# A fused attention and two-layer feed-forward kernel: VectorE in emission order after the attention, the second layer's block sums in the accumulators, the first layer's last products added by DMA

## The chip, the cores and the metric

One core of one Trainium2 chip. The metric is the device time of one execution in microseconds (us). The engines are TensorE (PE; its weight loads are PEld), VectorE (DVE), ScalarE (ACT), GpSimd (POOL) and SyncE (SP), which here only issues DMAs; POOL issues DMAs too, those that add to their target among them.

## The reference

```python
scores = scale * np.matmul(q, k.transpose(0, 1, 3, 2))         # 2 x 8 heads, 768 tokens, 64 wide
...                                                             # bias by distance, local and global keys kept
a = np.exp(scores - max); a = a / (a.sum(-1) + 1e-09)
x = np.matmul(a, v) -> reshaped to (1536, 512)
h = x @ w_in;  x = (h * (1 / (1 + np.exp(-h)))) @ w_out         # layer 0: 512 -> 2048 -> 512
h = x @ w_in2; out = (h * np.clip(h + 3, 0, 6) / 6) @ w_out2    # layer 1: 512 -> 2048 -> 512
```

The weights lie in memory as 64-bit floats.

## The kernel before

**Numbers.** Every matmul operand is split into a high half in a reduced 32-bit format (made by ACT) and a low half, the rest (made by DVE), and every product is three matmuls: high by high, high by low, low by high. A weight is loaded raw by SP (tile `raw`, two buffers) and *decoded* into a 32-bit float by a chain of small steps in 128x512 pieces: absolute value on ACT (L103), then on DVE clamp, shift, sign, power (L987 to L1004), scale (L129), add (L134), then the high half on ACT (L145) and the low half on DVE (L148). The load of the piece after the next is issued when a piece has been scaled.

**Stages.** The attention fills the first 130 us or so, and the first chunk of the feed-forward runs between its matmuls. Each layer is cut into 8 *chunks* of 256 hidden columns, written (layer, chunk). The 1536 tokens are three *blocks* of 512. An *H piece* (`h_piece`, 12 matmuls) gives 128 hidden rows for one block; ACT and DVE make the gated value and its halves from it (`gate_tile`: activation L529/L531, gate L536, `gh` L539, `gl` L542). A *Y piece* (`y_piece`, 6 matmuls) multiplies it by `w_out`; its results are summed over the chunks in the accumulators `acc[l, i]` (tiles `y0`, `y1`, `y2`): ACT copies a result to a staging tile `st` (three buffers, two results each), and POOL issues a DMA that adds it to `y` (L685). The last chunk of layer 0 is added by DVE instead (L695), and its sums are scaled and split into `xh` and `xl`, the input of layer 1.

**Fast chunks.** An ordinary chunk computes the H values of blocks 0 and 1 in 48 matmuls. A *fast* chunk needs 42: seven products of six matmuls (`product`, banks `psP_a`, `psP_b`, `psP_c`) of sums of weight quarters (`sums`) and sums of token blocks. The latter are made once per layer by `block_sums`: four differences of 128x1024 (L632), two on DVE (`V`) and two on POOL (`G`), and the halves T2, T3, T4 of three results, and a fourth that is written over the input of block 1. They work on whole copies of blocks 0 and 1 (`whole_blocks`, tiles `xf`), in layer 0 the sum of the two halves by two DMAs (SP, then an adding one on POOL), in layer 1 a copy of the accumulator. In a fast chunk two products are combined by DVE's addition into `u` (L595).

**Order.** The program is one list, `stream`, of H pieces, products and Y pieces, one per loop step `n`; the Y pieces of a block stand between the H pieces or products of a later one. `at(n, f)` puts an operation ahead of step n, `rests` and `late` put one behind it, `slots` holds the decode steps at fixed distances ahead of the chunk that needs the weights. PE, ACT and POOL work in just the order in which this loop emits (`manual_schedule`); DVE's and SP's orders are chosen by the library's scheduler from the dependencies. Each engine takes its instructions strictly in its order and waits at one whose inputs are not there.

```python
def fast(l, c):
    return c > (2, 0)[l]
...
for l, c, loop in ((0, 1, 5), (1, 0, 1)):
    if n == when(first_piece[l, c]) + loop:
        block_sums(l, n, when(first_piece[l, c + 2 - l]) - 7)
```

So layer 0 makes its block sums in chunk (0,1), and all chunks of layer 1 but the first are fast.

## Time and profile before

| | us |
|---|---|
| runs | 657.25, 653.9, 656.02; median 656.02 |
| the profiled execution | 653.48 |
| its span, first to last instruction | 651.7 |
| PE busy | 620.8 (95%) |
| DVE busy | 538.4 (83%) |
| ACT busy | 413.1 (63%) |
| POOL busy | 166.3 (26%) |
| mean granted clock of PE | 0.990 |

Shares of busy time are means over stages with different limits, so the views below are cut to stretches. A timeline gives start, duration, engine, line, operation, what is written and read, and in brackets the idle time of the engine before it and what ended that. Rows of one engine overlap a little at their ends: what an operation costs its engine is the distance from its start to the next one's.

### The profile page before, as it was taken

How to read it: one execution, taken by the hardware profiler on the slowest of the kernel's cores; microseconds unless marked ns; L12 is line 12 of the kernel's file. 1: busy time of each engine (PE TensorE's matmuls, PEld its weight loads, DVE VectorE, ACT ScalarE, POOL GpSimd, SP SyncE). 2: the span in 40 equal slices, each digit the busy share in tenths (PEclk: the TensorE clock that was granted, in tenths of full speed). 3: DMA queues.
4: the chain of work that ended last, by engine and by line, in shares of the span. 5: the costliest groups of instructions: out<-in, count | busy, mean ns of one | idle time of the engine just before them, and what ended most of it. 6: DMA issues, size and time to landing. Idle time of an engine off the chain costs nothing.

```text
span 651.7 us, 9793 instructions
## 1 busy us (share of the span) xinstructions
PE 620.8 (95%) x3208; PEld 500.2 (77%) x3208; DVE 538.4 (83%) x1173; ACT 413.1 (63%) x885; POOL 166.3 (26%) x229
## 2 busy tenths in 40 slices
PE   5989999999699999999999996999999999999996
PEld 3657777788588778888888884778888888888885
DVE  5899889945977888979887999989979797979553
ACT  4787778743555666666666653856757576666760
POOL 2776666662211111111111012001111211111110
PEclk9999999999899999999999997999999999999999
DMA  7555645358367668777777540235877677776544
GB/s 172 131 145 140 140 125 127 87 181 159 77 150 162 139 152 187 177 174 165 169 162 159 132 162 33 65 97 134 186 166 175 160 183 166 168 172 135 104 98 165
DMA packets 80762, 94.17 MB, mean 145 GB/s; under 512 B 55360, under 2 KB 55360, under 8 KB 80448
## 3 DMA queue, kind: packets, MB, share of 16 engines
q0 software_dynamic: 11424, 39.85, 34.0%
q1 hardware_dynamic: 69280, 53.63, 27.4%
q8 instruction: 27, 0.44, 0.3%
q14 instruction: 31, 0.25, 0.1%
HBM read 46.27 MB, written 3.15 MB: 76 GB/s over the span
## 4 chain that ended last, share of the span: by engine, by line
PE 74%; DVE 15%; DMA 6%; issue 2%; ACT 1%; SPq 1%; POOL 1%; POOLq 0%; DVEq 0%; ACTq 0%
PE psY L666 33%; PE psH L510 15%; PE psP_b L578 6%; PE psP_a L578 4%; PE psP_c L578 4%; PE psS L388 3%; PE psT L416 3%; PE psO L435 3%; PE psA L331 2%; DMA xf<-xl 2%; DMA xf<-xh 1%; DVE xl L607 1%; DVE da L999 1%; DMA raw<-in_moe_w_in_dram 1%; DVE gl L542 1%
## 5 line engine op out<-in xcount | busy, mean ns | idle before, releaser
L685 POOL DMA_DIRECT2D y<-st x72 | 61.7, 857 | 366.1 <-ACT st L682 356.3
L682 ACT COPY st<-psY 128x512 f32<-128x512 f32 x144 | 84.6, 587 | 57.3 <-PE psY L666 51.7
L510 PE MATMUL psH<-xh,wih 128*128 128x512 f32 (+1 forms) x200 | 76.8, 384 | 0.0
L510 PE MATMUL psH<-xh,wil 128*128 128x512 f32 (+1 forms) x200 | 76.2, 381 | 0.0
L510 PE MATMUL psH<-xl,wih 128*128 128x512 f32 (+1 forms) x200 | 76.2, 381 | 0.0
L666 PE MATMUL psY<-gh,woh 128*128 128x512 f32 (+1 forms) x160 | 62.1, 388 | 2.9 <-ACT gh L539 2.9
L666 PE MATMUL psY<-gl,woh 128*128 128x512 f32 (+1 forms) x160 | 61.5, 384 | 2.4 <-DVE gl L542 2.4
L539 ACT CAST gh<-g 128x512 fp32r<-128x512 f32 (+1 forms) x74 | 45.3, 612 | 25.9 <-DVE g L536 25.8
L666 PE MATMUL psY<-gh,wol 128*128 128x512 f32 (+1 forms) x160 | 61.1, 382 | 0.0
L398 ACT ACTIVATE z<-z,mn 128x256 f32<-128x256 f32 (+1 forms) x96 | 46.5, 486 | 22.0 <-DVE mn L394 17.4
L407 POOL TENSOR_SCALAR z<-z,sm 128x256 f32<-128x256 f32 (+1 forms) x96 | 48.3, 517 | 44.2 <-DVE sm L405 16.1
L666 PE MATMUL psY<-woh,gh 128*128 128x512 f32 x136 | 53.9, 396 | 5.6 <-ACT gh L539 5.5
L542 DVE TENSOR_TENSOR gl<-g,gh 128x512 fp32r<-128x512 f32 (+1 forms) x68 | 46.6, 685 | 11.1 <-ACT gh L539 10.5
L536 DVE SCALAR_TENSOR_TENSOR g<-a,psH 128x512 f32<-128x512 f32 (+1 forms) x50 | 33.1, 662 | 26.7 <-ACT a L529 17.8
L666 PE MATMUL psY<-woh,gl 128*128 128x512 f32 x136 | 53.8, 395 | 0.9 <-DVE gl L542 0.8
L666 PE MATMUL psY<-wol,gh 128*128 128x512 f32 x136 | 53.6, 394 | 0.0
L103 ACT ACTIVATE da<-raw 128x512 f32<-128x512 f32 x64 | 43.0, 671 | 5.2 <-DMA raw<-in_moe_w_in_dram 5.2
L987 DVE TENSOR_SCALAR da<-da 128x512 f32<-128x512 f32 x64 | 30.6, 479 | 18.7 <-ACT da L103 18.7
L529 ACT ACTIVATE a<-psH 128x512 f32<-128x512 f32 (+1 forms) x30 | 17.1, 570 | 44.8 <-PE psH L510 44.8
L999 DVE SCALAR_TENSOR_TENSOR da<-raw,da 128x512 int32<-128x512 int32 x64 | 44.3, 693 | 1.4 <-DVE sm L404 0.2
L510 PEld LDWEIGHTS psH<-xh,wih 128*128 128x128 f32 x200 | 37.6, 188 | 7.8 <-issue 1.0
L510 PEld LDWEIGHTS psH<-xh,wil 128*128 128x128 f32 x200 | 37.5, 188 | 6.6
(170 smaller groups left out, 1607.1 us busy)
## 6 DMA issues: line engine op xcount, KB each, us to landing
y<-st POOLq DMA_DIRECT2D x72, 512.0 KB, 5.0
raw<-in_moe_w_in_dram SPq DMA_DIRECT2D x32, 512.0 KB, 4.1
raw<-in_moe_w_out_dram SPq DMA_DIRECT2D x32, 512.0 KB, 4.7
rk<-in_k_dram SPq DMA_DIRECT2D x32, 96.0 KB, 2.6
rq<-in_q_dram SPq DMA_DIRECT2D x32, 96.0 KB, 3.1
rv<-in_v_dram SPq DMA_DIRECT2D x32, 96.0 KB, 2.7
out_dram<-y SPq DMA_DIRECT2D x12, 256.0 KB, 2.0
xf<-xh SPq DMA_DIRECT2D x2, 1024.0 KB, 6.7
```

Source lines behind the costliest of these rows:

```text
L103: nc.scalar.activation(out=t["a"], in_=raws[n][:, :, 1].bitcast(F32), func=AF.Abs)
L398: nc.scalar.activation(out=z[:, h, :w], in_=z[:, h, :w], func=AF.Exp, bias=mn[:, h:h + 1], scale=-1.0, accum_out=sm[:, h:h + 1])
L407: nc.gpsimd.tensor_scalar(out=z[:, h, :w], in0=z[:, h, :w], scalar1=sm[:, h:h + 1], scalar2=1.0, op0=ALU.mult, op1=ALU.mult)
L510: nc.tensor.matmul(ps, a[:, kt, js], x[:, kt, n0:n1], start=n == 0, stop=n == 3 * KT - 1)
L536: nc.vector.scalar_tensor_tensor(out=g, in0=t["a"], in1=ps, op1=ALU.mult, **op)
L539: nc.scalar.copy(gh[:, j, :], t["g"])
L542: (nc.vector if ready[0] else nc.gpsimd).tensor_tensor(out=gl[:, j, :], in0=t["g"], in1=gh[:, j, :].bitcast(F32), op=ALU.subtract)
L578: nc.tensor.matmul(ps, a[:, 2 * k + q, f * P:(f + 1) * P], x, start=p in (1, 5) and n == 0, stop=n == 5, skip_group_check=True)
L666: nc.tensor.matmul(ps[:, :rhs.shape[1]], lhs, rhs, start=n == 0, stop=n == 3 * FC - 1)
L682: nc.scalar.copy(st[:, m % 2, :], part)
L685: late.setdefault(now[0] + 1, []).append(lambda: nc.gpsimd.dma_start(y, st, accum_op=ALU.add))
L999: nc.vector.scalar_tensor_tensor(out=ai, in0=w1, scalar=-0x40000000, in1=ai, op0=ALU.bitwise_and, op1=ALU.bitwise_or)
```

## The change

DVE, too, works in emission order from the end of the attention on. The block sums of layer 0 are made in chunk (0,2) instead of (0,1), those of layer 1 in chunks (1,0) and (1,1), all on DVE; layer 1's are made in the old accumulators themselves, and the first sums of the new accumulators are held in the two large tiles until then and copied over by `first_sums`. So chunk (1,1) is an ordinary one. Layer 0's last products go through `st` and the adding DMA as all others do, and a pair of results is scaled and split 6 to 3 steps later. At the layer change the pieces stand in a new order.

```diff
@@ -154,7 +154,7 @@
 
     def fast(l, c):
 
-        return c > (2, 0)[l]
+        return c > (2, 1)[l]
 
     terms = {}
 
@@ -612,34 +612,38 @@
             at(n, first)
         at(n + 1, second)
 
-    def whole_blocks(l, b):
-
-        T[l, b] = late_pool.tile([P, KT, FB], F32, name=f"xf{l}{b}", tag=("ws", "g1")[b])
-        if l == 0:
-            h, o = (x.bitcast(F32)[:, :, b * FB:(b + 1) * FB] for x in (xh, xl))
-            nc.sync.dma_start(T[l, b], h)
-            nc.gpsimd.dma_start(T[l, b], o, accum_op=ALU.add)
-        else:
-            nc.sync.dma_start(T[l, b], acc[0, b])
+    def whole_block(b):
+
+        T["x", b] = late_pool.tile([P, KT, FB], F32, name=f"xf{b}", tag=("g1", "ws")[b])
+        h, o = (x.bitcast(F32)[:, :, b * FB:(b + 1) * FB] for x in (xh, xl))
+        nc.sync.dma_start(T["x", b], h)
+        nc.gpsimd.dma_start(T["x", b], o, accum_op=ALU.add)
 
     def block_sums(l, n, n1):
 
-        b0, b1 = T[l, 0], T[l, 1]
+        b0, b1 = (T["x", b] if l == 0 else acc[0, b] for b in range(2))
         b11, b12, b21, b22 = b0[:, :2, :], b1[:, :2, :], b0[:, 2:, :], b1[:, 2:, :]
         for k in (2, 3, 4):
             T[k] = [late_pool.tile([P, 2, FB], F32R, name=f"t{k}{x}{l}", tag=f"t{k}{x}") for x in "hl"]
         t1 = late_pool.tile([P, 2, FB], F32, name=f"t1f{l}", tag="u")
-        tt = lambda e, out, a, b: e.tensor_tensor(out=out, in0=a, in1=b, op=ALU.subtract)
-        V, G = nc.vector, nc.gpsimd
+        sub = lambda out, a, b: nc.vector.tensor_tensor(out=out, in0=a, in1=b, op=ALU.subtract)
         scale = (1.0, 0.5)[l]
-        at(n, lambda: tt(V, t1, b12, b11))
-        at(n + 1, lambda: tt(V, b11, b22, t1))
-        at(n + 2, lambda: tt(G, b12, b22, b12))
-        at(n + 3, lambda: tt(G, b21, b21, b11))
-        split(n + 3, *T[2], b11, scale)
-        split(n + 5, *T[3], b12, scale)
-        split(n + 7, *T[4], b21, scale)
+        at(n, lambda: sub(t1, b12, b11))
+        at(n + 2, lambda: sub(b12, b22, b12))
+        at(n + 3, lambda: sub(b11, b22, t1))
+        split(n + 4, *T[3], b12, scale)
+        split(n + 6, *T[2], b11, scale)
+        at(n + 8, lambda: sub(b21, b21, b11))
+        split(n + 9, *T[4], b21, scale)
         split(n1, *(x[:, :2, FB:2 * FB] for x in (xh, xl)), t1, scale)
+        if l:
+            at(n + 10, first_sums)
+
+    def first_sums():
+
+        for b in range(2):
+            acc[1, b] = xpool.tile([P, FB // P, DM], F32, name=f"y1_{b}", tag=f"y{b}")
+            nc.gpsimd.dma_start(acc[1, b], T["y", b])
 
     def parts(n0, n1):
 
@@ -667,6 +671,11 @@
                 n += 1
         at_ = 0
         for i, ts, size in parts(n0, n1):
+            if (l, c) == (1, 0) and i < 2:
+                if m == 0:
+                    T["y", i] = late_pool.tile([P, FB // P, DM], F32, name=f"yf{i}", tag=("g1", "ws")[i])
+                nc.scalar.copy(T["y", i][:, m, :], ps)
+                continue
             if (l, i) not in acc:
                 acc[l, i] = xpool.tile([P, KT, FB] if l == 0 else [P, FB // P, DM], F32, name=f"y{l}_{i}", tag=f"y{i}")
             a, part = (acc[l, i][:, m, ts], ps[:, at_:at_ + size]) if l == 0 else (acc[l, i][:, m, :], ps[:, :DM])
@@ -674,29 +683,27 @@
             if c == 0:
                 nc.scalar.copy(a, part)
                 continue
-            if c < NCH - 1:
-
-                if m % 2 == 0:
-                    staged[0] = late_pool.tile([P, 2, FB], F32, name=f"st{l}_{c}_{i}_{m}", tag="st", bufs=3)
-                st = staged[0]
-                nc.scalar.copy(st[:, m % 2, :], part)
-                if m % 2:
-                    y = acc[l, i][:, m - 1:m + 1, :]
-                    late.setdefault(now[0] + 1, []).append(lambda: nc.gpsimd.dma_start(y, st, accum_op=ALU.add))
-                    if c == NCH - 2 and l == 1:
-                        for j in range(2):
-                            at(now[0] + 9 + j, lambda j=j: nc.scalar.mul(y[:, j, :], y[:, j, :], 1.0 / 6.0))
-                continue
-            if l == 1:
+            if c == NCH - 1 and l == 1:
                 nc.vector.scalar_tensor_tensor(out=a, in0=part, scalar=1.0 / 6.0, in1=a, op0=ALU.mult, op1=ALU.add)
                 r = n0 + m * P
                 nc.sync.dma_start(out[r:r + P, :], a)
                 continue
-            nc.vector.tensor_tensor(out=a, in0=part, in1=a, op=ALU.add)
-            hi, lo = (x[:, m, n0:n1] for x in (xh, xl))
-            split(now[0] + 1, hi, lo, a, 0.5)
-            if m == KT - 1 and i < 2:
-                at(now[0] + 1, lambda: whole_blocks(1, i))
+
+            if m % 2 == 0:
+                staged[0] = late_pool.tile([P, 2, FB], F32, name=f"st{l}_{c}_{i}_{m}", tag="st", bufs=3)
+            st = staged[0]
+            nc.scalar.copy(st[:, m % 2, :], part)
+            if m % 2 == 0:
+                continue
+            y, n = acc[l, i][:, m - 1:m + 1, :], now[0]
+            late.setdefault(n, []).append(lambda: nc.gpsimd.dma_start(y, st, accum_op=ALU.add))
+            if c == NCH - 2 and l == 1:
+                for j in range(2):
+                    at(n + 9 + j, lambda j=j: nc.scalar.mul(y[:, j, :], y[:, j, :], 1.0 / 6.0))
+            if c == NCH - 1:
+
+                wait = ((6, 6), (5, 5), (4, 3))[i][m // 2]
+                split(n + wait, *(x[:, m - 1:m + 1, n0:n1] for x in (xh, xl)), y, 0.5)
 
 
     stream, first_piece = [], {}
@@ -715,16 +722,19 @@
             stream += [h[0]] + y[:2] + [h[1]] + y[2:]
             before = Y(l, c, 1) + Y(l, c, 2)
             continue
-        if l:
-
-            stream += before[:4]
-            before = before[4:]
+        if (l, c) == (1, 0):
+
+            h = H(l, c, 0) + H(l, c, 1) + H(l, c, 2)
+            stream += before[:6]
             first_piece[l, c] = len(stream)
+            stream += [h[0]] + before[6:] + h[1:4] + Y(l, c, 0) + h[4:5] + Y(l, c, 1)[:2] + h[5:] + Y(l, c, 1)[2:]
+            before = Y(l, c, 2)
+            continue
         for tk in blocks(l, c):
             hs = [(h_piece, l, c, tk, j) for j in range(FC)]
-            ys = before or [None] * 4
+            ys, before = (before or [None] * 4)[:4], before[4:]
             stream += [hs[0], *ys[:2], hs[1], *ys[2:]]
-            before = [(y_piece, l, c, tk, m) for m in range(KT)]
+            before += [(y_piece, l, c, tk, m) for m in range(KT)]
     stream += before
 
 
@@ -758,34 +768,39 @@
         rk_()
         rq_()
         biases(0)
-    with tc.manual_schedule(engines={mybir.EngineType.PE, mybir.EngineType.Activation, mybir.EngineType.Pool}):
-        todo = {when(i): f for i, f in enumerate(stream)}
-        late_pool = None
-        for n in range(when(len(stream) - 1) + 2):
+    todo = {when(i): f for i, f in enumerate(stream)}
+
+    def loop(n):
+        now[0] = n
+        attention_loop(n)
+        f = todo.get(n)
+        if f:
+            f[0](*f[1:])
+        if APOS == 2:
+            transposes(n)
+        for f in late.pop(n, []) + slots.pop(n, []):
+            f()
+
+    E = mybir.EngineType
+    end = len(seq) + LAG + 2
+    with tc.manual_schedule(engines={E.PE, E.Activation, E.Pool}):
+        for n in range(end):
             if n == len(seq) + LAG:
                 ready[0] = 1
-            if n == len(seq) + LAG + 2:
-
-                first_half.close()
-                late_pool = second_half.enter_context(tc.tile_pool(name="late", bufs=1, side="right", reuse_waits="tile"))
-                for b in range(2):
-                    whole_blocks(0, b)
+            loop(n)
+    with tc.manual_schedule(engines={E.PE, E.Activation, E.Pool, E.DVE}):
+
+        first_half.close()
+        late_pool = second_half.enter_context(tc.tile_pool(name="late", bufs=1, side="right", reuse_waits="tile"))
+        for b in range(2):
+            whole_block(b)
+        for n in range(end, when(len(stream) - 1) + 2):
             if n == when(first_piece[0, 3]):
                 ready[0] = 2
-            now[0] = n
-            for l, c, loop in ((0, 1, 5), (1, 0, 1)):
-                if n == when(first_piece[l, c]) + loop:
-                    block_sums(l, n, when(first_piece[l, c + 2 - l]) - 7)
-            now[0] = n
-            attention_loop(n)
-            f = todo.get(n)
-            if f:
-                f[0](*f[1:])
-            if APOS == 2:
-                transposes(n)
-            for f in late.pop(n, []) + slots.pop(n, []):
-                f()
-
+            for l, c, early in ((0, 2, 0), (1, 1, 6)):
+                if n == when(first_piece[l, c]) - early:
+                    block_sums(l, n, n + early + 12)
+            loop(n)
             if n == PRE + 60:
                 general = nc.values_load(flag[0:1, 0:1], min_val=0, max_val=2)
     second_half.close()
```

DVE after the attention, chunk (0,1): `g` is a gated value, `gl` its low half, `da`, `de`, `dc` are decode steps, `t1f` and `xf` the block sums. Before:

```order
L536 SCALAR_TENSOR_TENSOR g0_1_0_0_2622<-a0_1_0_0_2619,psH0_1_0_0_2604 128x512
L632 TENSOR_TENSOR t1f0_2685<-xf01_2551,xf00_2548 128x1024
L542 TENSOR_TENSOR gl0_1_0_2618<-g0_1_0_0_2622,gh0_1_0_2617 128x512
L632 TENSOR_TENSOR xf00_2548<-xf01_2551,t1f0_2685 128x1024
L536 SCALAR_TENSOR_TENSOR g0_1_0_1_2666<-a0_1_0_1_2658,psH0_1_0_1_2645 128x512
```

And of the change:

```order
L536 SCALAR_TENSOR_TENSOR g0_1_0_0_2625<-a0_1_0_0_2622,psH0_1_0_0_2607 128x512
L1014 SCALAR_TENSOR_TENSOR da8_2594<-raw8_1828,da8_2594 128x512
L542 TENSOR_TENSOR gl0_1_0_2621<-g0_1_0_0_2625,gh0_1_0_2620 128x512
L1019 TENSOR_SCALAR de8_2646<-da8_2594 128x512
L129 SCALAR_TENSOR_TENSOR dc8_2663<-raw8_1828,de8_2646 128x512
L536 SCALAR_TENSOR_TENSOR g0_1_0_1_2669<-a0_1_0_1_2661,psH0_1_0_1_2648 128x512
```

The two differences have left the place between the gates, and decode steps stand there.

ACT of the change at the layer change, from the copy of block 0's last product to the scaling half of its last pair (`st` are copies of products, `da` and `wih`, `woh` first and high halves of weight pieces, `xh` the scaling half):

```order
L695 COPY st0_7_0_2_4607<-psY0_7_0_3_4612 128x512
L145 CAST wih8_4544<-dc33_4576 128x512
L695 COPY st0_7_1_0_4631<-psY0_7_512_0_4624 128x512
L103 ACTIVATE da35_4638<-raw35_4498 128x512
L695 COPY st0_7_1_0_4631<-psY0_7_512_1_4640 128x512
L604 ACTIVATE xh_80<-y0_0_1618 128x2x512
L695 COPY st0_7_1_2_4659<-psY0_7_512_2_4652 128x512
L103 ACTIVATE da36_4662<-raw36_4578 128x512
L695 COPY st0_7_1_2_4659<-psY0_7_512_3_4665 128x512
L145 CAST woh8_4674<-dc34_4634 128x512
L695 COPY st0_7_2_0_4686<-psY0_7_1024_0_4679 128x512
L604 ACTIVATE xh_80<-y0_0_1618 128x2x512
```

Before, there were no copies here, and each result had its own scaling half right behind DVE's addition.

DVE of the change at the same place, from block 0's first pair-wide low half to its second, which layer 1's first H piece needs (the load of piece 36, `raw36`, is issued behind the scale step of piece 34, four rows ahead of these):

```order
L607 SCALAR_TENSOR_TENSOR xl_81<-y0_0_1618,xh_80 128x2x512
L1014 SCALAR_TENSOR_TENSOR da35_4638<-raw35_4498,da35_4638 128x512
L1002 TENSOR_SCALAR da36_4662<-da36_4662 128x512
L148 TENSOR_TENSOR wol8_4675<-dc34_4634,woh8_4674 128x512
L1019 TENSOR_SCALAR de35_4689<-da35_4638 128x512
L1008 TENSOR_SCALAR da36_4662<-da36_4662 128x512
L129 SCALAR_TENSOR_TENSOR dc35_4702<-raw35_4498,de35_4689 128x512
L1014 SCALAR_TENSOR_TENSOR da36_4662<-raw36_4578,da36_4662 128x512
L607 SCALAR_TENSOR_TENSOR xl_81<-y0_0_1618,xh_80 128x2x512
```

The second `xl` stands behind the first steps of piece 36. Before, DVE's additions (L695) and the single low halves stood here, and POOL's differences lay beside them.

## Rows read from the trace of the kernel before

**Rows 1.** Busy us by engine (xcount), PEclk, DMA, GB/s; 440 to 640 us
```profile
440.00:640.00 200.00, 199.85 (x882) 165.46 (x882) 162.23 (x287) 132.76 (x235) 30.88 (x36) 1.00 0.69 155
```

**Rows 2.** Chain that ended last: start, us, what, xcount
```profile
310.76 1.36 PE psP_a L578 x6
...
333.88 2.72 PE psY L666 x12
```

**Rows 3.** Waits of PE from 130 us on: total us, times, longest
```profile
PE psY L666 <- ACT gh L539: 8.4, 2, 5.5
PE psY L666 <- DVE gl L542: 3.2, 3, 2.0
```

**Rows 4.** PE timeline, first stop: start, duration, line, [idle before <-releaser]
```profile
162.15 0.39 PE L666 MATMUL psY<-gh,woh 128*128 128x512 f32 x1
...
165.86 0.50 PE L666 MATMUL psY<-gh,woh 128*128 128x512 f32 x1 [2.87 <-ACT gh L539]
...
171.72 0.40 PE L510 MATMUL psH<-xh,wih 128*128 128x512 f32 x1
```

**Rows 5.** PE timeline, second stop
```profile
392.20 0.39 PE L666 MATMUL psY<-woh,gh 128*128 128x512 f32 x1
...
398.54 0.80 PE L666 MATMUL psY<-woh,gh 128*128 128x512 f32 x1 [5.50 <-ACT gh L539]
...
400.56 0.80 PE L666 MATMUL psY<-woh,gl 128*128 128x512 f32 x1 [0.80 <-DVE gl L542]
...
403.63 0.39 PE L510 MATMUL psH<-xh,wih 128*128 128x512 f32 x1
```

**Rows 6.** Windows as in rows 1, around the first stop
```profile
165.00:168.00 3.00, 0.50 (x1) 0.19 (x1) 2.97 (x4) 2.00 (x4) 2.00 (x1) 1.00 0.00 0
168.00:172.00 4.00, 3.61 (x10) 2.92 (x11) 3.90 (x7) 1.10 (x2) 0.00 (x0) 0.57 0.20 44
```

**Rows 7.** DVE timeline, first stop
```profile
159.41 1.23 DVE L632 TENSOR_TENSOR t1f<-xf,xf 128x1024 f32<-128x1024 f32 x1 [4.91 <-DMA xf<-xl]
...
161.15 3.41 DVE L632 TENSOR_TENSOR xf<-xf,t1f 128x1024 f32<-128x1024 f32 x1
164.48 0.67 DVE L536 SCALAR_TENSOR_TENSOR g<-a,psH 128x512 f32<-128x512 f32 x1
```

**Rows 8.** POOL timeline, first stop
```profile
160.72 2.75 POOL L632 TENSOR_TENSOR xf<-xf 128x1024 f32<-128x1024 f32 x1 [10.51 <-DVE t1f L632]
```

**Rows 9.** DVE timeline, second stop
```profile
390.40 2.89 DVE L607 SCALAR_TENSOR_TENSOR xl<-y,xh 128x512 fp32r<-128x512 f32 x1
...
397.16 0.67 DVE L536 SCALAR_TENSOR_TENSOR g<-a,psH 128x512 f32<-128x512 f32 x1
```

**Rows 10.** DVE timeline in a fast chunk
```profile
322.30 0.69 DVE L595 TENSOR_TENSOR u<-psP_c,u 128x512 f32<-128x512 f32 x1
322.90 0.42 DVE L987 TENSOR_SCALAR da<-da 128x512 f32<-128x512 f32 x1
...
329.62 0.69 DVE L542 TENSOR_TENSOR gl<-g,gh 128x512 fp32r<-128x512 f32 x1
```

**Rows 11.** POOL timeline, second stop (two merged in one row)
```profile
389.27 6.21 POOL L632 TENSOR_TENSOR xf<-xf 128x1024 f32<-128x1024 f32 x2 [25.06 <-DVE t1f L632]
```

**Rows 12.** DVE timeline, 1024-wide low half
```profile
398.69 1.21 DVE L607 SCALAR_TENSOR_TENSOR t2l<-xf,t2h 128x1024 fp32r<-128x1024 f32 x1
```

**Rows 13.** Staging tile st: durations ns min/median/max, DMA landing
```profile
L682 ACT COPY st<-psY x144: 566/589/595, 169.7 to 624.4; 128x512 f32<-128x512 f32 x144
...
DMA to landing us min/median/max: 4.5/5.0/7.4
```

**Rows 14.** ACT timeline, 1024-wide scaling half
```profile
390.51 1.06 ACT L604 ACTIVATE t2h<-xf 128x1024 fp32r<-128x1024 f32 x1 [1.89 <-DVE xf L632]
```

**Rows 15.** Weight tile raw, 165 to 652 us: landing of its loads
```profile
DMA to landing us min/median/max: 3.1/4.4/7.1
```

**Rows 16.** DMA issues: xcount, KB each, median us to landing
```profile
xf<-xl POOLq DMA_DIRECT2D x2, 1024.0 KB, 9.6
```

## The prediction

> **What bounds the kernel now.** I read the busy shares by stretch first, then TensorE's waits, then the two places they lie in, then who held the work that TensorE waited for. In steady running TensorE (PE) has no idle time: busy 199.85 of 200 us, while VectorE (DVE) is busy 162.23 [rows 1]. There six matmuls of 512 columns take 1.36 us, that is 0.227 us each [rows 2]. So only two things can move the time after the attention: the number of matmuls, and the stops of PE. After 130 us the waits are few: 8.4 us for `gh` and 3.2 us for `gl`, the two halves of the gated value [rows 3]. They lie in two places.
>
> The first stop is the Y pair that starts at 162.15: twelve matmuls until 171.72, 9.57 us instead of 2.72, a loss of **6.85 us** [rows 4]. The second is the pair from 392.20 to 403.63: 11.43 instead of 2.72, a loss of **8.71 us** [rows 5]. Not all of a stop is waiting. After the first the granted clock is 0.57 for 4 us, near the lower of its two levels (1.2 and 2.4 GHz) [rows 6], and matmuls run slower there. A stop avoided gives both back.
>
> Who held the work? At the first stop DVE stood idle 4.91 us before the first difference of the block sums, until the landing of `xf<-xl`; then the second difference took 3.41 us, and the gate that PE needed came only at 164.48 [rows 7]. GpSimd (POOL) was in its own 1024-wide difference from 160.72 [rows 8]. At the second stop a 512-wide DVE operation took 2.89 us instead of 0.69 [rows 9, 10], the one behind it about as long, and the gate was put off to 397.16 [rows 9]; just then POOL ran its two differences, 6.21 us [rows 11]. A DVE operation that meets POOL's subtraction takes four times as long here.
>
> **The change, part by part.**
> *Layer 0's block sums move from chunk (0,1) to (0,2)*, all four on DVE. The first stop had no other cause than these differences standing in front of two gates: I take it as gone, **-6.85 us**. The loads of `xf` start where they did; the last landed at 159.4 [rows 7], some 20 us before the new place. What they cost at the new place: chunk (0,2) has 6 H pieces of 2.72 and 12 Y pieces of 1.36, 32.6 us of PE. DVE's work there, by the steps at which rows follow each other (0.60 us for a 512-wide operation, 0.34 to 0.46 for a short one [rows 10], 1.14 for a 1024-wide one, whose row is 1.21 [rows 12]): 4 differences and 4 low halves 9.1, gates and their low halves 7.2, one chunk's decode with its sums about 14: 30.4 of 32.6 us. Followed step by step, each low half is ready one to two pieces before its Y piece, so I cost it at nothing; if a miss occurs it is a microsecond or two.
>
> *Four subtractions leave POOL*: with them the stretched DVE operations [rows 9] go, and nothing new stands on POOL but DMA issues.
>
> *Chunk (1,1) becomes an ordinary one*: 48 matmuls instead of 42, 6 x 0.227 = **+1.36 us**, all on PE, which has no idle time to hide it.
>
> *Layer 0's last products*: 12 additions of DVE (0.60 each) become 12 copies on ACT (0.59 [rows 13]) and 6 accumulating DMAs, which land 4.5 to 7.4 us after issue, median 5.0 [rows 13]. Their pair-wide scaling halves wait 6 to 3 steps of the stream. The critical one is block 0, the last pair. Let its PE end be t = 0. Six Y pieces follow, 8.16 us, then layer 1's first H piece, whose eighth matmul needs this low half: t = 9.75. The DMA alone would do: copy done at 0.7, landed at 5.7, then 1.06 on ACT and 1.21 on DVE [rows 12, 14], t = 8. But ACT takes its work in the order of emission, DVE now too, and between stands the decode for chunk (1,1): ACT reads its first weight piece only two steps after the load for it is issued, since chunk (1,0) now begins two Y pieces later in the stream while (1,1) follows 16 pieces on. That load is issued after a DVE step that I place at t = 2.4 (gate, sign, low half, power, low half of a weight, scale, after the H piece). Weight loads land in 3.1 to 7.1, median 4.4 us [rows 15]: t = 6.8. Then ACT: that piece, a copy, a high half, each near 0.6, to 8.7; then DVE: a low half, two short ones, two more 512-wide, to 11.2, and the low half for PE, t = 12.4. So PE stops **2.65 us** where 8.71 were lost. Bounds: with the fastest load DVE's chain still ends 1.2 us late; with the slowest 5.4, and with the clock falling as it did at the second stop (8.71 less the idle 5.50 and 0.80 [rows 5], 2.4 us) 7.8. I take 2.65 without a fall, since after the first stop's wait of 2.87 us the clock was still 1.00 [rows 4, 6].
>
> The later blocks have more cover: three H pieces stand before layer 1's first Y piece, and the halves for blocks 1 and 2 fall due 10 us after their products.
>
> *Layer 1's sums in the accumulators*: the two 1 MB copies onto the halves of `xf` go; two on POOL's queue appear (`first_sums`). The nearest row for that size on that queue is 9.6 us [rows 16]. Behind them on POOL wait the next accumulations only; their staging buffers are three deep, so ACT is held up after some 16 us. Nothing.
>
> *DVE in emission order in the fast chunks*: 11 of them remain. Here DVE must wait, with everything behind it, at the addition of `u` (L595). In the trace it starts at 322.30 and the last low half that the next Y pair needs starts at 329.62, done by 330.30; the pair starts at 333.88, its fourth matmul 0.7 later [rows 2, 10]. Between the two the new order has two 512-wide operations more, 1.2 us: some 3 us stay. Nothing.
>
> **Sum.** 653.48 (the profiled execution; span 651.7) - 6.85 - (8.71 - 2.65) + 1.36 = 641.9 us. The profiled execution lies 2.5 us below the median of the runs, 656.02; on the median I forecast **644.5 us**, 1.8% less.
>
> **Rivals.**
> 1. *The second stop stays.* The load or ACT is later than I place it, and the clock falls: 7.8 us lost instead of 2.65, 649.7. For it: everything there now runs through two queues in order. Against: DVE loses its stretched operations. Chance 0.15.
> 2. *DVE in order becomes the bound* (the other side). Place: L595 in each fast chunk; the DVE waits for ACT's copy of the product before, and 9 us of work stands behind it. Until it is 3.3 us late nothing happens; beyond that each us costs 11. It eats the gain of 11.5 us at 1.05 us per chunk and ends over 0.5% slower from 1.35 us per chunk, 4.65 us late: 659.5 or more. For it: DVE is busy 81% even now [rows 1], and an order by readiness is given up. Against: in the trace DVE's order in these chunks is nearly the emission order already, with idle time left. Chance 0.10, half of it slower, half within 0.5%.
> 3. *The first stop only moves*: DVE, 93% loaded in chunk (0,2), falls behind there by some 4 us, 648.5. Chance 0.05.
> 4. *Accumulating DMAs on POOL's queue land late beside a dense DVE.* If they took the 9.6 us of [rows 16], block 0's pair would land at t = 10.3 and its low half end near 12.7, and blocks 1 and 2 could each lose 1 to 2 us: 648. Chance 0.05. The Trainium skill says this in "SBUF — State Buffer", section "SBUF: two separate sides": a DMA issued from GpSimd needs descriptors that GpSimd cannot write while VectorE, in a two-port mode, holds the port pair that both share. By that rule this rival would be the likely one; the trace so far speaks against, since the 72 such DMAs (of two copies each) never landed later than 7.4 us beside a DVE that was busy four fifths of the time [rows 1, 13].
>
> **How the numbers follow.** Forecast 0.65 (640 to 647), rivals as above. About 0.5%, 3.3 us, is what a measurement of this kernel can tell from no change. Faster: all but rival 2 and a little of rival 1: 0.88; same 0.07; slower 0.05. The range: down to 639, where the second stop costs only its lower bound, 1.2 us, and the small stops at the start of the fast stretch shrink too; up to 651, which takes in rivals 1, 3 and 4.
>
> **What would show it.** Right: no PE idle time over 0.5 us in the first H and Y pieces of chunk (0,1), eight 1024-wide differences on DVE at about 1.2 us each and none on POOL; at the layer change one PE wait of 1 to 5 us in the first H piece, ended by DVE's `xl`, with ACT idle before it for a weight load; 552 H matmuls of 512 columns. Wrong: PE gaps that recur every 31 us, or a granted clock below 1 for more than 5 us at the layer change.

## The result, and the profile after

The changed kernel takes **646.67 us** (median of 4 runs, 646.44 to 647.96), the kernel before 656.0 beside it (653.9 to 657.25): a ratio of 0.9861, 95% interval 0.9835 to 0.9887, so 1.4% less. The forecast was 644.5, range 639 to 651. The profiled execution is 646.63, span 644.7 (653.48 and 651.7 before). Its busy times and shares, from the page:

```profile
PE 619.8 (96%) x3214; PEld 500.1 (78%) x3214; DVE 514.5 (80%) x1151; ACT 416.9 (65%) x886; POOL 161.9 (25%) x233
```

PE is busy for nearly as long as before (620.8); the time went out of its stops. The medians differ by 9.3 us, the two profiled executions by 6.85, and only the latter have traces to explain it.

How much of that lies behind the attention is read from two matmuls, the first of layer 0's first H piece and the last of the program. The PE timeline of the kernel before:

```profile
141.22 0.44 PE L510 MATMUL psH<-xh,wih 128*128 128x384 f32 x1
...
645.71 0.39 PE L666 MATMUL psY<-woh,gl 128*128 128x512 f32 x1
```

and of the changed kernel:

```profile
140.94 0.44 PE L510 MATMUL psH<-xh,wih 128*128 128x384 f32 x1
...
638.90 0.39 PE L670 MATMUL psY<-woh,gl 128*128 128x512 f32 x1
```

From the one to the other it is 504.49 us before and 497.96 after: 6.53 less. I call this the *feed-forward length*; below it stands for every run, since it leaves out the opening, which varies by itself (last section). The same stretch holds the stops, given as *PE time lost*: the distance from the start of one matmul to the next, less 0.227 us for a matmul of 512 columns. Such a sum is good to some 0.2 us. Before, 18.4 us were lost in all: 6.84 and 8.71 in the two stops and 0.5 to 0.8 at each of four small ones. After, it is 10.5. PE's waits in the changed kernel from 130 us on, where [rows 3] had 8.4 and 3.2 us:

```profile
PE psH L510 <- ACT xh L604: 2.9, 1, 2.9
PE psH L510 <- DVE xl L607: 1.5, 1, 1.5
PE psP_b L578 <- ACT psP_b L583: 1.1, 2, 0.5
PE psY L670 <- DVE gl L542: 0.5, 2, 0.4
```

No wait for `gh` is left: the first stop [rows 4] is gone, and `gl` waits half a microsecond where it waited 3.2. The differences that had stood in front of the gates [rows 7], by line (minimum, median and maximum duration in ns, first and last start in us), are now all on DVE, none stretched. Layer 0's four:

```profile
L629 DVE TENSOR_TENSOR xf<-xf x2: 1211/1214/1218, 185.5 to 197.2; 128x1024 f32<-128x1024 f32 x2
L629 DVE TENSOR_TENSOR t1f<-xf,xf x1: 1219/1219/1219, 182.1 to 182.1; 128x1024 f32<-128x1024 f32 x1
L629 DVE TENSOR_TENSOR xf<-xf,t1f x1: 1220/1220/1220, 187.9 to 187.9; 128x1024 f32<-128x1024 f32 x1
```

The last of these, `xf<-xf,t1f`, took 3.41 us in [rows 7]. Layer 1's four take 1.22 each. The large wait that is left is a new one, at the layer change. PE there:

```profile
374.50 0.39 PE L510 MATMUL psH<-xh,wih 128*128 128x512 f32 x1
...
378.96 0.79 PE L510 MATMUL psH<-xh,wih 128*128 128x512 f32 x1 [2.93 <-ACT xh L604]
...
381.25 0.79 PE L510 MATMUL psH<-xl,wih 128*128 128x512 f32 x1 [1.50 <-DVE xl L607]
...
395.32 0.39 PE L670 MATMUL psY<-woh,gh 128*128 128x512 f32 x1
```

From 374.50 to 395.32 stand 60 matmuls, 13.6 us of work in 20.8: 7.2 lost. 4.43 of it is idle, the rest slow matmuls (0.79 instead of 0.39). The windows show why (columns as in [rows 1]):

```profile
374.00:378.00 4.00, 2.02 (x9) 1.33 (x8) 0.94 (x2) 2.19 (x5) 0.77 (x1) 1.00 0.57 116
378.00:384.00 6.00, 3.54 (x8) 2.46 (x9) 5.27 (x9) 2.55 (x4) 0.95 (x2) 0.50 0.92 206
384.00:388.00 4.00, 4.00 (x17) 3.27 (x16) 2.35 (x4) 2.68 (x5) 0.00 (x0) 0.89 0.72 170
```

A granted clock of 0.50, the lower level (1.2 GHz), for 6 us; it fell within PE's idle time of 2.93 us. Now who held PE. ACT's timeline:

```profile
375.81 0.66 ACT L103 ACTIVATE da<-raw 128x512 f32<-128x512 f32 x1 [4.52 <-DMA raw<-in_moe_w_in_dram]
...
377.83 1.07 ACT L604 ACTIVATE xh<-y 128x1024 fp32r<-128x1024 f32 x1
```

DVE's, which waits for ACT in turn:

```profile
368.29 0.69 DVE L129 SCALAR_TENSOR_TENSOR dc<-raw,de 128x512 f32<-128x512 uint32 x1
...
376.50 0.43 DVE L1002 TENSOR_SCALAR da<-da 128x512 f32<-128x512 f32 x1 [3.83 <-ACT da L103]
...
379.98 1.22 DVE L607 SCALAR_TENSOR_TENSOR xl<-y,xh 128x1024 fp32r<-128x1024 f32 x1
```

And SP's, which issues the load:

```profile
369.04 0.38 SPq L87 DMA_DIRECT2D raw<-in_moe_w_in_dram  x1
```

ACT stands 4.52 us for a load of chunk (1,1) (piece 36, counted through the program), which nobody needs yet, and the halves of `x`, for which PE waits, stand behind it on ACT and DVE. That load was issued at 369.04 and landed at 375.72. The DMA view of 366 to 376.5 us (count, KB each, median us to landing) shows what it ran beside:

```profile
y<-st POOLq DMA_DIRECT2D x2, 512.0 KB, 7.2
raw<-in_moe_w_in_dram SPq DMA_DIRECT2D x1, 512.0 KB, 6.7
```

Two adding DMAs, issued at 367.43 and 370.14, overlap it, and the load took 6.7 us where [rows 15] had a median of 4.4.

### The profile page after: what moved, and what is told of

It reads as the page before. It is cut to its first block, busy times and chain, and to the rows that moved or that the text cites. A ratio compares the mean times of both kernels' runs of the same rounds, so it can differ in the third digit from the quotient of the medians.

```text
span 644.7 us, 9784 instructions
## 1 busy us (share of the span) xinstructions
PE 619.8 (96%) x3214; PEld 500.1 (78%) x3214; DVE 514.5 (80%) x1151; ACT 416.9 (65%) x886; POOL 161.9 (25%) x233
## 4 chain that ended last, share of the span: by engine, by line
PE 83%; DVE 9%; DMA 4%; ACT 2%; issue 2%; SPq 0%; POOL 0%; DVEq 0%; ACTq 0%; POOLq 0%
PE psY L670 37%; PE psH L510 21%; PE psP_b L578 6%; PE psP_c L578 4%; PE psP_a L578 4%; PE psS L388 3%; PE psO L435 3%; PE psT L416 3%; DMA raw<-in_moe_w_in_dram 2%; PE psA L331 2%; DVE z L394 1%; DMA rk<-in_k_dram 1%; DVE da L1014 1%; DVE sm L404 1%; DVE pt L419 1%
## 5 line engine op out<-in xcount | busy, mean ns | idle before, releaser
L699 POOL DMA_DIRECT2D y<-st x78 | 67.2, 862 | 369.6 <-ACT st L695 364.5
L695 ACT COPY st<-psY 128x512 f32<-128x512 f32 x156 | 91.3, 585 | 44.0 <-PE psY L670 39.0
L510 PE MATMUL psH<-xh,wih 128*128 128x512 f32 (+1 forms) x216 | 83.8, 388 | 3.0 <-ACT xh L604 2.9
L510 PE MATMUL psH<-xl,wih 128*128 128x512 f32 (+1 forms) x216 | 83.0, 384 | 1.5 <-DVE xl L607 1.5
L510 PE MATMUL psH<-xh,wil 128*128 128x512 f32 (+1 forms) x216 | 82.9, 384 | 0.0
L542 DVE TENSOR_TENSOR gl<-g,gh 128x512 fp32r<-128x512 f32 (+1 forms) x70 | 48.0, 686 | 10.9 <-ACT gh L539 8.9
L670 PE MATMUL psY<-wol,gh 128*128 128x512 f32 x144 | 56.0, 389 | 0.0
L536 DVE SCALAR_TENSOR_TENSOR g<-a,psH 128x512 f32<-128x512 f32 (+1 forms) x54 | 35.8, 664 | 24.4 <-ACT a L529 18.2
L510 PEld LDWEIGHTS psH<-xh,wih 128*128 128x128 f32 x216 | 40.8, 189 | 12.1 <-ACT xh L604 3.4
L510 PEld LDWEIGHTS psH<-xl,wih 128*128 128x128 f32 x216 | 40.8, 189 | 9.1 <-DVE xl L607 2.0
L510 PEld LDWEIGHTS psH<-xh,wil 128*128 128x128 f32 x216 | 40.8, 189 | 7.3
```

The lines of the kernel that those rows point to most:

```text
L510: nc.tensor.matmul(ps, a[:, kt, js], x[:, kt, n0:n1], start=n == 0, stop=n == 3 * KT - 1)
L536: nc.vector.scalar_tensor_tensor(out=g, in0=t["a"], in1=ps, op1=ALU.mult, **op)
L542: (nc.vector if ready[0] else nc.gpsimd).tensor_tensor(out=gl[:, j, :], in0=t["g"], in1=gh[:, j, :].bitcast(F32), op=ALU.subtract)
L670: nc.tensor.matmul(ps[:, :rhs.shape[1]], lhs, rhs, start=n == 0, stop=n == 3 * FC - 1)
L695: nc.scalar.copy(st[:, m % 2, :], part)
L699: late.setdefault(n, []).append(lambda: nc.gpsimd.dma_start(y, st, accum_op=ALU.add))
```

## The experiments

Eleven runs; each table entry is worked out as above. All lengths and losses are from the one profiled execution of each.

| | median us | ratio to before, interval | feed-forward length | lost at first stop | at layer change | in all |
|---|---|---|---|---|---|---|
| before | 656.0 | | 504.49 | 6.84 | 8.71 | 18.4 |
| changed | 646.67 | 0.9861 (0.9835 to 0.9887) | 497.96 | 0 | 7.1 | 10.5 |
| e1 | 643.59 | 0.9811 (0.9777 to 0.9845) | 492.54 | 0 | 1.85 | 5.4 |
| e2 | 648.98 | 0.9899 (0.9864 to 0.9935) | 498.21 | 0 | 7.7 | 10.9 |
| e3 | 645.34 | 0.9836 (0.9805 to 0.9867) | 495.71 | 4.8 | 1.3 | 8.5 |
| e4 | 656.98 | 1.0009 (0.9986 to 1.0032) | 505.84 | 7.6 | 8.6 | 18.5 |
| e5 | 648.03 | 0.9894 (0.9859 to 0.9928) | 498.59 | 0 | 7.8 | 11.2 |
| e6 | 651.46 | 0.9941 (0.9921 to 0.9960) | 500.00 | 4.9 | 6.5 | 13.9 |
| e7 | 645.24 | 0.9853 (0.9824 to 0.9881) | 495.48 | 0 | 5.0 | 8.1 |
| e8 | 645.65 | 0.9855 (0.9831 to 0.9879) | 494.08 | 0 | 2.2 | 7.0 |
| e9 | 641.46 | 0.9775 (0.9743 to 0.9807) | 491.35 | 0 | 1.3 | 4.1 |
| e10 (as e1) | 644.46 | 0.9825 (0.9796 to 0.9855) | 493.02 | 0 | 2.4 | 5.7 |
| e11 (as changed) | 647.35 | 0.9869 (0.9840 to 0.9898) | 498.25 | 0 | 7.6 | 10.8 |

**e1: the decode of chunk (1,1) later.** If ACT's wait for the load is the cause, reading it some steps later must give the stop back.

```diff
-ahead = ... else ((20, 15, 11, 6), (18, 14, 9, 2))[fast(*chunks[i])][j]
+ahead = ... else (16, 12, 9, 5)[j] if chunks[i] == (1, 1) else ((20, 15, 11, 6), (18, 14, 9, 2))[fast(*chunks[i])][j]
```

> The changed kernel with one table entry more: the decode of chunk (1,1)'s weights starts 4, 3, 2 and 1 steps later (16, 12, 9, 5 ahead of the chunk instead of 20, 15, 11, 6), so that ACT reads weight piece 36 behind the scaling half of block 0 and not ahead of it. Theory (the stop at the layer change is the load of piece 36, at which ACT and DVE wait in order with block 0's last halves behind them): the stop of 7.2 us shrinks to under 1.5 us, about 640 us. Rival (the stop is the landing of the adding DMAs themselves, 6.3 us for block 0's last pair): the stop stays at 5 to 7 us, 646 us.

The loss at the layer change falls from 7.1 to 1.85 (expected under 1.5) and the feed-forward length by 5.4 us. One window of the changed kernel (columns as in [rows 1]):

```profile
374.00:393.00 19.00, 14.57 (x53) 10.94 (x53) 13.53 (x21) 10.76 (x17) 2.58 (x3) 0.82 0.73 162
```

the same window of e1:

```profile
374.00:393.00 19.00, 17.80 (x77) 13.99 (x76) 14.85 (x23) 12.93 (x20) 2.57 (x3) 1.00 0.77 169
```

and what PE still waits for there in e1:

```profile
PE psH L510 <- DVE xl L607: 0.8, 1, 0.8
```

The clock no longer falls there: with the wait went the slow stretch behind it. The load is no quicker, it lands 6.5 us after its issue; ACT only asks for it later. What remains is the adding DMA: block 0's last lands 6.8 us after its issue, and the low half with it. The median gained 3.1 us, not 5.4, and is 643.59, not the 640 expected: in the profiled execution the opening is 2.6 us longer than in the changed kernel's (first H matmul at 143.52 against 140.94). e10 returns to that.

**e2: layer 0's last products added by DVE again**, in the changed kernel; the pair is split at the same steps.

```diff
+            if c == NCH - 1:
+                nc.vector.tensor_tensor(out=a, in0=part, in1=a, op=ALU.add)
+                if m % 2:
+                    wait = ((6, 6), (5, 5), (4, 3))[i][m // 2]
+                    split(now[0] + wait, ...)
+                continue
```

> The changed kernel, but layer 0's last products are added by DVE as before (12 additions of 128x512 out of PSUM, no copies on ACT, no adding DMAs there); the pair-wide halves stay where they are. Theory (load of piece 36): ACT still waits for that load at the layer change, but the load no longer shares the queues with two adding DMAs and lands in about 4 us instead of 6.7, so PE stops 1 to 3 us without a fall of the clock: 641 to 643 us. Rival (adding DMAs' own landing): no wait of ACT there and no stop, 639 to 640 us. Second rival (DVE is the scarce engine there): 12 x 0.6 us more on DVE keeps the stop at 6 us or more, 646 us.

The load is quick again without adding DMAs beside it, 3.5 us in the DMA view of 369 to 377:

```profile
raw<-in_moe_w_in_dram SPq DMA_DIRECT2D x1, 512.0 KB, 3.5
```

But the stop stays, 7.7 us, as the second rival had it. DVE is now the engine that is late, busy 23.70 of 25 us from 360 to 385 (columns as in [rows 1]):

```profile
360.00:385.00 25.00, 20.91 (x83) 16.61 (x82) 23.70 (x41) 8.81 (x13) 0.00 (x0) 0.89 0.22 71
```

**e7: both edits of e1 and e2 together**, which takes the load out of the way and asks for the price of the adds alone.

> The changed kernel with the decode of chunk (1,1) some steps later and with the last products of layer 0 added by VectorE (the two edits of the earlier runs together). Theory: with the load of piece 36 out of the way, what is left at the layer change is VectorE's own work, four adds of a product more for each block, and the adds by DMA are needed to keep it short: TensorE loses 3 to 5 us there, 644.5 to 647 us. Rival: with the decode moved away VectorE has the time, and an add on it ends sooner than an adding DMA that lands 6.8 us after its issue: under 1.5 us lost there (1.85 with the adding DMAs), 643 or less.

5.0 us lost, against 1.85 with the adding DMAs; PE waits once, for DVE:

```profile
PE psH L510 <- DVE xl L607: 3.1, 1, 3.1
```

So moving the adds off DVE is worth some 3 us at the layer change, and makes the load beside them land some 3 us later; only with the decode moved too does the first come out whole.

**e3: DVE's order left to the scheduler again**, all else as changed.

```diff
-    with tc.manual_schedule(engines={E.PE, E.Activation, E.Pool, E.DVE}):
+    with tc.manual_schedule(engines={E.PE, E.Activation, E.Pool}):
```

> The changed kernel with DVE's order left to the library's scheduler after the attention, as before the change; everything else of the change stays. Theory (the gain comes from where the block sums stand and from POOL's subtractions going, not from DVE's emission order): within 3 us of the changed kernel, 644 to 650 us. Rival (emission order itself brings the gain): 651 us or more, with new stops of PE behind DVE.

The net is nearly nothing (645.34 against 646.67), so the forecast of the time held; its theory did not, since the net is made of two terms of opposite sign. The first stop is back with 4.8 us, though the sums are emitted in chunk (0,2): the scheduler puts them ahead of the decode of (0,1), and DVE stands. Its timeline:

```profile
161.60 1.23 DVE L629 TENSOR_TENSOR t1f<-xf,xf 128x1024 f32<-128x1024 f32 x1 [4.79 <-DMA xf<-xl]
```

The layer change loses only 1.3, as the scheduler had the scale of piece 34 earlier, which releases the load of piece 36: issued 1.8 us before the end of block 0's last product, not 2.7 us behind it, and landed at 376.05, before ACT asked for it at 377.92. The issue, on SP's timeline, and the first H matmul of layer 1, which follows that end by 8.16 us:

```profile
371.33 0.38 SPq L87 DMA_DIRECT2D raw<-in_moe_w_in_dram  x1
...
381.25 0.39 PE L510 MATMUL psH<-xh,wih 128*128 128x512 f32 x1
```

**e5: the block sums back in chunk (0,1)**, in emission order, all on DVE: place and order separated.

```diff
-for l, c, early in ((0, 2, 0), (1, 1, 6)):
+for l, c, early in ((0, 1, -5), (1, 1, 6)):
...
-                    block_sums(l, n, n + early + 12)
+                    block_sums(l, n, when(first_piece[0, 3]) - 7 if l == 0 else n + early + 12)
```

> The changed kernel, with layer 0's block sums called again in chunk (0,1), five steps in, as before the change; VectorE stays in emission order and all differences stay on VectorE. Theory: what removed the first stop is that the differences are emitted a chunk later, once the two copies of x have landed, and that emission order holds them there. With them back in (0,1), VectorE should stand at the first difference until the copies land, and the decode queued behind it is late: a stop of 3 to 6 us of TensorE in (0,1) comes back (4.8 when the scheduler pulled them forward), the rest as in the changed kernel, 649.5 to 652.5 us. Rival: the stop was made by the scheduler's order and GpSimd's subtractions, not by the place; then under 1 us is lost there and the time stays at 646 to 647.5.

My theory fell. No stop comes back: in emission order the first difference comes after the decode steps that are due, when the copies of `x` have landed, and the others stand one by one between gates and decode:

```profile
159.64 0.42 DVE L1002 TENSOR_SCALAR da<-da 128x512 f32<-128x512 f32 x1
159.98 1.22 DVE L629 TENSOR_TENSOR t1f<-xf,xf 128x1024 f32<-128x1024 f32 x1
161.11 0.68 DVE L542 TENSOR_TENSOR gl<-g,gh 128x512 fp32r<-128x512 f32 x1
```

It starts without a wait, 18.5 us behind the first H matmul. In e3 it starts after 18.1 us, hardly sooner, but in the time that e3's DVE stood there, 4.79 us, e5's did a gate and two decode steps. With e3 this tells order from place: the scheduler's order loses 4.8 with the sums emitted in (0,2); emission order loses nothing with the sums in either chunk. With all differences on DVE, the order did it, not the move.

**e6: the kernel before without GpSimd's subtractions.**

```diff
-        V, G = nc.vector, nc.gpsimd
+        V, G = nc.vector, nc.vector
```

> The kernel before, with GpSimd's two subtractions of each block-sum group given to VectorE; order and places stay. Theory: GpSimd's subtractions slow VectorE beside them (2.89 us instead of 0.69 for one operation), which is some 2 us of the first stop and 2 to 4 of the second: TensorE loses about 4.8 in the first (6.84 before) and 4.5 to 6.5 in the second (8.71 before), 650 to 652.5 us. Rival: VectorE's own two operations of 1.2 us in their place and the order behind them cost as much as the contention did: 655 to 657.5.

4.9 and 6.5 us lost instead of 6.84 and 8.71: giving GpSimd's differences to DVE, which then has two more of them in each layer, takes 1.9 us from the first stop and 2.2 from the second, 4.1 of 15.6 us. DVE's second difference, 3.41 us in [rows 7], is an ordinary one, and the wait ahead of the first is still there:

```profile
160.58 1.23 DVE L632 TENSOR_TENSOR t1f<-xf,xf 128x1024 f32<-128x1024 f32 x1 [5.01 <-DMA xf<-xl]
161.72 0.68 DVE L542 TENSOR_TENSOR gl<-g,gh 128x512 fp32r<-128x512 f32 x1
162.32 1.22 DVE L632 TENSOR_TENSOR xf<-xf,t1f 128x1024 f32<-128x1024 f32 x1
```

**e4: chunk (1,1) ordinary in the kernel before**, nothing else (the second layer's sums then have a later due step).

```diff
-        return c > (2, 0)[l]
+        return c > (2, 1)[l]
-                    block_sums(l, n, when(first_piece[l, c + 2 - l]) - 7)
+                    block_sums(l, n, when(first_piece[l, (3, 2)[l]]) - 7)
```

> The kernel before with one part of the change alone: chunk (1,1) is an ordinary one, so layer 1's block sums, made where they were, are used one chunk later. Theory (PE bound): 6 matmuls more, 1.36 us; both stops stay; profiled execution 654 to 656 us. Rival (the ordinary chunk relieves DVE or the weight loads behind the layer change, where PE lost 1.5 us at the start of the first fast chunk): no change or up to 2 us faster.

The times can't tell it from no change. The two matmuls that bound the feed-forward can:

```profile
141.89 0.44 PE L510 MATMUL psH<-xh,wih 128*128 128x384 f32 x1
...
647.73 0.39 PE L666 MATMUL psY<-woh,gl 128*128 128x512 f32 x1
```

505.84 against 504.49: 1.35 us more, where six matmuls were to cost 1.36. There are six more of them in the trace; that the lengths agree to 0.01 us is chance, since the first stop came out 0.8 us longer here and the small ones 0.7 shorter together. No relief of the second stop is seen beside it.

**e8: e1, and the first pieces of chunks (0,4) and (1,3) later too**, against the small stops, at which ACT stands at a weight load ahead of the copy L583.

```diff
+... (16, 13, 9, 2)[j] if chunks[i] in ((0, 4), (1, 3)) else ...
```

> The changed kernel with the decode of chunk (1,1) some steps later and, besides, the first two pieces of chunks (0,4) and (1,3) two and one steps later (their places 16 and 13 steps ahead of their chunk instead of 18 and 14), so that ScalarE does not stand at a weight load ahead of the copy that starts the second product chain. Theory: of the four small stops (0.78, 0.98, 0.80, 0.79 us) about half goes; TensorE loses 3 to 4.5 us in all (5.39 without this edit), and the time is 642 to 643. Rival: the later pieces make the sums of weights late, and chunks (0,4) and (1,3) start with stops of 1 us or more each: 644.5 to 647.

The rival holds. The wait for the copy is gone, but that for `gl` grows to 2.9 us:

```profile
PE psY L670 <- DVE gl L542: 2.9, 2, 1.6
PE psH L510 <- DVE g L536: 1.0, 1, 1.0
```

**e9: emission order on DVE only until chunk (0,3)**, the scheduler from there on: each where e3 and e5 showed it to serve.

```diff
+    part = when(first_piece[0, 3])
     with tc.manual_schedule(engines={E.PE, E.Activation, E.Pool, E.DVE}):
...
-        for n in range(end, when(len(stream) - 1) + 2):
+        late_loop(PRE + 61, part)
+    with tc.manual_schedule(engines={E.PE, E.Activation, E.Pool}):
+        late_loop(part, when(len(stream) - 1) + 2)
```

> The changed kernel with VectorE in emission order only until chunk (0,3) begins, and left to the scheduler from there on. Theory: emission order is worth its gain in chunk (0,1), where a difference that waits for the copies of x must not stand ahead of the decode, and costs at the layer change, where the scheduler put the scale of piece 34 earlier and so the load of piece 36; with each where it serves, no stop of TensorE over 1 us in (0,1) or (0,2), 1.3 to 2 us lost at the layer change, some 0.5 to 0.8 us at each of the four small stops, 3.5 to 5 us in all (10.5 in the changed kernel, 8.5 with the scheduler throughout); 640 to 643 us, by when the clock rises in the opening. Rival: the scheduler's good order at the layer change hung on its order before; then 5 to 8 us are lost there again and the time is 645 to 648.

It has the lowest median and the shortest feed-forward of all: 641.46 us, ratio 0.9775 (the interval just overlaps that of e10), 4.1 us lost in all. Its DVE timeline has the scale of piece 34, and its PE timeline the first H piece of layer 1, at

```profile
365.72 0.69 DVE L129 SCALAR_TENSOR_TENSOR dc<-raw,de 128x512 f32<-128x512 uint32 x1
...
376.40 0.39 PE L510 MATMUL psH<-xh,wih 128*128 128x512 f32 x1
```

There are 10.7 us between them, where the changed kernel has 6.2 (368.29 and 374.50). That is the cover that the load lacked.

**e10 and e11: e1 and the changed kernel once more**, on the same chip as e9.

> The same kernel as in the first run with the later decode of chunk (1,1), with more rounds and beside the changed kernel on one chip. Theory: the layer change gives back 5 us of the changed kernel's 7.1 in every execution, and the opening up to the first step of layer 0 differs from execution to execution by some 3 us in either kernel; the median lies 3 to 5.5 us under that of the changed kernel, and the stop at the layer change stays under 2.2 us. Rival: the later decode itself makes the opening longer; then the first step again comes at 143.5 us (140.9 in the changed kernel) and the distance stays at 3 us or less.

> The changed kernel once more, as the neighbour of the two others of this call. Theory: 645 to 648 us, the stop at the layer change 6 to 8 us with a load of piece 36 that lands over 6 us after its issue; the first step of layer 0 comes at 140.5 to 144 us. Rival: the late landing was an accident of the one profiled execution; then the stop is 3 to 5 us here.

The stop at the layer change is 7.6 us in the changed kernel and 2.4 in e10 (a little over the 2.2 expected), so neither was an accident; the medians lie 2.9 us apart (expected 3 to 5.5), the feed-forward lengths 5.2. In e10 the opening was as short as in the changed kernel, so the later decode does not lengthen it. Why the medians differ by less than the feed-forward lengths is not settled: e10's runs spread from 641.87 to 647.56, and the one with a trace is the fastest of them. The opening is the only part seen to vary so far, by 2.7 us (last section).

## Why the prediction came out as it did

- **First stop, -6.85 us: right in size, and its cause half named.** I put it down to the differences standing in front of two gates, and its removal to their move into (0,2). e5 shows that the move was not needed: with the differences all on DVE, emission order removes it in either chunk, and without emission order the move does not (e3). GpSimd's subtractions were 1.9 us of it (e6), not the greater part.
- **Chunk (1,1) ordinary, +1.36: right**, 1.35 in e4, and 552 H matmuls of 512 columns, as forecast.
- **Second stop, 2.65 lost instead of 8.71: the term that was mis-sized**, 7.1 to 7.6 in two executions. The mechanism was the one described: a load for (1,1), ACT's read of it in order, the halves of `x` behind. With t = 0 at 366.34, the end of block 0's last product, the H piece begins at t = 8.16 as forecast, and the load's issue at t = 2.70 (forecast 2.4). But it landed at 9.38, not 6.8, as it took 6.7 us and not the median of 4.4; the low half then ended at t = 14.9, not 12.4. PE waited twice, 2.93 us for the high half on ACT and 1.50 for the low half, where one wait had been forecast. And the clock fell, for 2.7 us more, which I had put in the bounds alone. The reason for that was no good: I took the clock to stay up since it was still 1.00 after the first stop's wait, but the next row of [rows 6] has 0.57. A clock below 1 for more than 5 us here was also my own sign of being wrong, and it came. Both terms stood in the bounds ("7.8"), and the median was the wrong choice: the change itself puts two adding DMAs beside that load, and e2 measures it without them, 3.5 us. (The lower bound, 1.2, is 1.35 by the terms that stand beside it.)
- **Sum.** With 7.1 in place of 2.65 the sum on the profiled execution is 646.4; measured 646.63. In the feed-forward the same terms come to 7.1 us, of which 6.53 arrived: the four small stops, which I left out, grew by 0.6 in all. That I was off by only 2.2 us on the median is luck: I had added 2.5 for the distance from the profiled execution to the median, and after the change that distance is 0.04. Carrying it over had no ground. It may lie in the opening, which varies by as much; with one trace of the kernel before, that is not shown.
- **What no run takes apart.** The new order of the pieces at the layer change and layer 1's sums in the accumulators were priced at nothing. No run leaves either out; beside the terms above, the loss at the layer change among them, 0.2 us at most is left for them.
- **Rival 1** (the second stop stays, 7.8 lost), to which I gave 0.15, is what came at the layer change, and for the reason it names: the load was later than placed and the clock fell. Its 649.7, less the 2.5 us that should not have been added, is 647.2; measured 646.67.
- **Rival 2** (DVE binds in the fast chunks) did not occur. DVE's timeline in a fast chunk, answering to [rows 10]:

```profile
315.48 0.69 DVE L595 TENSOR_TENSOR u<-psP_c,u 128x512 f32<-128x512 f32 x1 [3.27 <-ACT u L589]
...
324.35 0.68 DVE L542 TENSOR_TENSOR gl<-g,gh 128x512 fp32r<-128x512 f32 x1
```

  and the Y pair behind it, from the chain of waits (start, us):

```profile
327.07 2.72 PE psY L670 x12
```

  The last low half is done at 325.03, needed at 327.07 + 0.68: 2.7 us of margin, forecast some 3. PE is not idle there.
- **Rival 3** (the first stop moves into (0,2)): nothing is lost there.
- **Rival 4** (adding DMAs late beside a dense DVE). Landing of the adding DMAs, minimum, median and maximum, where [rows 13] had 4.5, 5.0 and 7.4:

```profile
DMA to landing us min/median/max: 4.5/4.8/8.0
```

  The median did not rise, with DVE busy 80% of the span. Of the 78, 18 took over 6 us. They lie all over the feed-forward, and each ran beside another adding DMA and for 2.4 us or more beside a weight load; DVE was less busy beside them (59% in the mean) than beside the other 60 (85%). The rule of the Trainium skill, "SBUF — State Buffer", section "SBUF: two separate sides", by which a VectorE operation in a two-port mode keeps GpSimd from writing the descriptors of the DMAs that it issues, is not seen in these landings. A load issued by SP was slowed as much, by 3.2 us between e2 and the changed kernel. At the critical place the adding DMA did land later than forecast, at t = 7.4 and not 5.7, but still ahead of the load. With the load out of the way, in e1, it is what PE waits for, 0.8 us.

## What to carry to other kernels

Where an engine takes its work strictly in order, ask of each instruction in front of an urgent one whether what it waits for has landed, and put a read of a load that is not yet needed behind the work that is; that was worth 5 us of the feed-forward here, and 3 us of the median, by one line of four numbers. Price a transfer by what the change itself runs beside it, not by the median of the trace before. And an order chosen by hand is not better everywhere: emission order gained 4.8 us at one place and cost 5.8 at another (e3), and taking it only where it gains gave the lowest time measured.

## What the runs showed of the hardware that was not expected

**A load and adding DMAs go slower beside one another.** The same 512 KB load took 3.5 us without adding DMAs near it (e2) and 6.7 beside two of them. The adding ones took 4.5 to 8.0 in the changed kernel, and each of the 18 that took over 6 us ran beside a load and another adding one; which of the two costs more is not taken apart.

**The clock did not follow the length of a wait alone.** After 2.87 us of idle time at the first stop before, the granted clock was still 1.00 [rows 4, 6], and it fell only at 168.0, 2.1 us after PE had resumed and within its next wait; in the idle 2.93 us at the layer change it fell before PE resumed, and the first matmul already took 0.79.

**The opening varies by 2.7 us between executions of the same kernel.** The PE timeline of e1, four transposes near 21 us in one row and the first H matmul:

```profile
21.75 1.12 PE L416 MATMUL psT<-ident,z 128*128 128x128 f32 x4
...
143.52 0.44 PE L510 MATMUL psH<-xh,wih 128*128 128x384 f32 x1
```

and of e10, the same program:

```profile
20.88 0.66 PE L416 MATMUL psT<-ident,z 128*128 128x128 f32 x4
...
140.86 0.44 PE L510 MATMUL psH<-xh,wih 128*128 128x384 f32 x1
```

The same four matmuls take 1.12 or 0.66 us. It goes with the clock. The trace's record of the granted clock begins at 24.5 us in e1 and at 19.7 in e10, at the upper level (2.4 GHz). Before its first entry the column of the windows reads 1.00 whatever the clock is, so there only the matmuls show it: one of 128 columns takes 0.42 us before that moment and 0.27 behind it, in either run. In e1 the clock then falls once more, to the lower level for 3.4 us, after PE had stood idle for 0.80 us. The windows of 31 to 35 us, e1 and then e10 (columns as in [rows 1]):

```profile
31.00:35.00 4.00, 3.93 (x26) 2.72 (x28) 2.89 (x15) 2.77 (x10) 2.84 (x7) 0.57 0.36 92
31.00:35.00 4.00, 4.00 (x40) 2.74 (x39) 3.81 (x18) 3.77 (x15) 3.45 (x6) 1.00 0.55 176
```

All thirteen profiled executions follow this. In the seven whose record begins by 21.6 us and has no fall in the opening, the first H matmul comes at 140.8 to 141.5; in the six with a later rise or such a fall, at 141.9 to 144.1. What makes the clock rise sooner or later in the same program is open. The difference is as large as several of the effects measured here, which is why the feed-forward length stands beside each median.
